# Fourier mixing and a gated feed-forward block on one core: the order of the opening, and the first chunk's second matmul

## The chip, the cores and the metric

The kernel runs on one core of a Trainium2 chip. The core has a matmul engine (PE, with a separate row PEld for loading its stationary operand), a vector engine (DVE), an activation engine (ACT), a general-purpose engine (POOL) and a queue engine (SP) that here only starts transfers. Each engine works through its own list of instructions in order and waits on semaphores for the others. Transfers between the chip's memory and the on-chip buffers are started from SP's and POOL's lists. The metric is the device time of one execution in microseconds (us); lower is better.

## The reference

The input `x` has 8 batches of 3008 positions with 256 channels, in fp32. The reference takes the real part of a Fourier transform along both axes and feeds every position through a gated block with 1536 hidden units:

```python
X = np.fft.fft(x, axis=1)
X = np.fft.fft(X, axis=2)
y = X.real.reshape(24064, 256)
g = y @ w_gate
gelu = 0.5 * g * (1.0 + erf(g / sqrt(2)))
out = (gelu * (y @ w_val)) @ w_out
```

## The kernel before

**Transform.** The 3008 positions are split as 94 x 32. `x` of a batch is loaded twice: forward (rows 32 p + j) and mirrored (an indirect gather, "M" below). A fold adds and subtracts the two (`fold_ops`, L216 to L220), so that only 17 columns j are left; a piece (j0, nj) is nj of them. Stage 1 (`s1`, L467) multiplies the folded pieces with a matrix G of cosines and sines, four groups of j by two halves, and copies each result to A (L473 on ACT, L475 on DVE). `ch` (L489) multiplies A with signed identities II and gives Z; `tp_e`, `tp_o` and `tp_y` (L544, L549, L569) multiply Z with a small table TP and give EO (even and odd parts) and EB. The channel transform is not done on the data: it is folded into the weights by `make_w` (L417), which multiplies the raw weights with a table CW, and `make_yw` adds a rank-one term.

**Feed-forward.** A batch has three chunks of up to 512 column pairs; each chunk has 12 blocks of 128 hidden units. One block is one slot of the order written out in `feed()`, so there are 8 x 3 x 12 = 288 slots. In slot i PE does the two gate matmuls of block i (`l1_gate`), one more for the mirrored gate of block i - 1 (`l1_gate2`), the value matmul of block i (`l1_value`) and the second one of block i - 1 (`l1_value2`), all at L622. ACT applies the gelu twice (L638, L647). DVE makes `ve` (L656), the product for the forward sign (L667) and `v` (L669). POOL makes the product for the mirrored sign (L671). Both products go to `h`.

**Layer 2.** `l2_piece(ci, sub, sign, f0)` (L695) is four matmuls over four hidden blocks; a chunk has 4 sub-blocks x 2 signs x 3 = 24 pieces. The six pieces of a sub-block share the one PSUM buffer with tag "o"; after the sixth, ACT copies it out (L714) and SP stores it. The list `pend` holds the pieces of the chunk just finished. Two are taken in each slot of the next chunk: the first after the value matmul, the second after `l1_value2`.

**Order.** Nothing is scheduled by a planner: the program order is written by hand. `opening()` holds the constants, the loads and the first batch up to the first gate. `plan()` gives for each slot the further work: `fill` (stage 1, `ch`, `tp`, loads, `make_w`) comes at the end of a slot, `pool` (folds of the next batch on POOL) before `l1_value2`. In the first chunk `fill` makes the rest of the weights in slots 0 to 7 and the rest of the first batch's transform in slots 7 to 16. `second_x` and its followers start the loads of the second batch in slots 0 to 5; folds of the second batch on POOL begin in slot 6. The loads of the third batch are started in slots 18 and 19.

**The lines that the change touches.** In `opening()` SP loads the forward part of `x` for j = 9 to 16 and 0 as fp32 (`stage`); POOL's list has first its index and constant rows, then the gathers and the casting loads of `x`, then w and w_out. DVE and ACT make the tables: G's phases (L314 to L261) and sines (L328 to L338), CW (L343 to L359), the identities (L363 to L366, on ACT) and TP (L371 to L388). `warm(n)` puts n matmuls without use on PE (L757). `keep2` is the factor with which `make_w` writes a third form of the odd gate weights ("minus", L427).

Of the kernel before, what the change touches and what calls it, by code (L numbers as in the profile page):

```python
# [28 lines left out]
def kernel(  # L29
# [17 lines left out]
    NK = 24  # L47
# [51 lines left out]
    def stage_tile():  # L99
        return work([NPX, 9, C], FP32, "h", 2, "x_stage")  # L100
# [89 lines left out]
    def fold_ops(b, j0, nj, eng):  # L190
# [3 lines left out]
        def fwd(c0, pat):  # L194
            if b == 0 and j0 not in range(1, 9):
                return _sub(stage[0], [[C, nj]] + pat, (j0 - 9 if j0 else 8) * C + c0, part_num=NP)
            if half:
                return _sub(xb[b], [[C, nj]] + pat, j0 * C + c0, part_num=NP)
            return _sub(raw_tile(FORWARD), [[C, nj]] + pat, j0 * C + c0, part_num=NP)
# [35 lines left out]
    sc_g = const_pool.tile([128, 2], FP32)  # L235
    row_j = const_pool.tile([128, NJ], FP32)
    row_k = const_pool.tile([128, NK], FP32)
    row_c, eye = (const_pool.tile([128, 128], FP32, name=f"row{i}") for i in range(2))
    par = const_pool.tile([1, 5, 128], FP32)
    one = const_pool.tile([1, 1], FP32)  # L240
# [8 lines left out]
    rd = work([128, 2 * NGP], FP32, "Z", 1, "rd")  # L249
# [5 lines left out]
    col_i = const_pool.tile([128, 2], FP32)  # L255
# [7 lines left out]
    def index_consts(i):  # L263
        idx, base = ((idx_x, NP - 1), (idx_0, NP))[i]
        nc.gpsimd.iota(col_i[:, i : i + 1], pattern=[[0, 1]], base=base, channel_multiplier=-1, **IOTA)
        if i:
            nc.gpsimd.memset(col_i[0:1, i : i + 1], 0.0)
        nc.gpsimd.tensor_scalar(idx, col_i[:, i : i + 1], 0.0, None, op0=ALU.max)

    def pool_consts():  # L270
# [4 lines left out]
        nc.gpsimd.iota(row_c, pattern=[[1, 128]], base=0, channel_multiplier=0, **IOTA)  # L275

    def pool_consts2():

        nc.gpsimd.iota(
            par[:, 0, :], pattern=[[1, 16], [0, 2], [32, 2], [0, 2]], base=1, channel_multiplier=0, **IOTA)
        for r, v in ((120, 0.0), (122, 32.0), (126, 16.0)):
            nc.gpsimd.memset(par[:, 0, r : r + 2], v)
        nc.gpsimd.iota(row_t, pattern=[[1, K1]], base=0, channel_multiplier=0, **IOTA)

    def vec_fills():
        nc.vector.memset(G[:, 0, 2 * NK :], 0.0)
        nc.vector.memset(G[:, 16, 0 : 2 * NK], 0.0)
        nc.vector.memset(one, 1.0)  # L290
# [13 lines left out]
    def vec_consts():  # L304
# [3 lines left out]
        nc.vector.tensor_scalar(col_e, col_h, -1.0, 1.0, op0=ALU.mult, op1=ALU.add)  # L308
        nc.vector.tensor_scalar(sc_g[:, 1:2], col_h, -TWO_PI, None, op0=ALU.mult)
        nc.vector.tensor_scalar(sc_g[:, 0:1], col_h, TWO_PI, -TWO_PI, op0=ALU.mult, op1=ALU.add)  # L310

    def g_phases():
        f, r, d = (_sub(t, [[1, 2 * NGP]], 0, part_num=NP) for t in (ff, rr, rd))
# [7 lines left out]
        nc.vector.tensor_scalar(f[:, NK:NGP], f[:, NGP + NK :], 0.25, None, op0=ALU.add)  # L321
        nc.vector.tensor_scalar(f[:, 0:NK], f[:, NGP : NGP + NK], 0.125, None, op0=ALU.add)
        reduced(d, r, f)

    def g_sin(j0, nj):
# [7 lines left out]
    def g_sin_ends():  # L333
# [3 lines left out]
        for h in range(2):  # L337
            nc.scalar.activation(  # L338
                _sub(G, [[1, NK]], h * NK), _sub(rd, [[1, NK]], 0, part_num=NP),
                AF.Sin, scale=sc_g[:NP, h : h + 1])  # L340

    def cw_phases():
        nc.vector.tensor_scalar(col_n0, col_p, 1.0 / C, None, op0=ALU.mult)  # L343
        nc.vector.tensor_scalar(cf[:, 0:128], row_c, col_n0, 0.25, op0=ALU.mult, op1=ALU.add)
        nc.vector.tensor_scalar(cf[:, 128:256], row_c, col_n0, 0.5, op0=ALU.mult, op1=ALU.add)
        reduced(cd[:, :], cr[:, :], cf[:, :])

    def cw_sin():
        nc.scalar.activation(_sub(CW, [[256, 2], [1, 128]], 0), cd[:, :], AF.Sin, scale=-TWO_PI)

    def cw_rest():


        nc.scalar.activation(CW[:, 0, 0, 0:1], col_e, AF.Copy)
        nc.scalar.activation(CW[:, 1, 0, 0:1], col_h, AF.Copy)
        for i, sign in enumerate((1.0, -1.0)):
            nc.scalar.activation(
                _sub(CW, [[256, 2], [2, 64]], 128 + i), _sub(CW, [[256, 2], [2, 64]], i), AF.Copy, scale=sign)
        nc.scalar.activation(CW[:, 1, 1, 0:1], col_h, AF.Copy)  # L359

    def identities():

        nc.scalar.activation(eye, row_c, AF.Abs, scale=-1.0, bias=col_p)  # L363
        nc.scalar.activation(II[:, 0, 0, :], eye, AF.Relu, scale=-1.0, bias=1.0)
        for i, sign in ((1, 1.0), (2, 1.0), (3, -1.0)):
            nc.scalar.activation(II[:, i // 2, i % 2, :], II[:, 0, 0, :], AF.Copy, scale=sign)  # L366

    def t_columns():
        ps = psum("v")
        for i in range(5):  # L370
            nc.tensor.matmul(ps[:, i : i + 1], par[:, i, :], one, start=True, stop=True)  # L371
        nc.vector.tensor_copy(parc, ps[:, 0:5])
        nc.vector.tensor_scalar(parc[:, 0:1], parc[:, 0:1], 1.0 / K1, None, op0=ALU.mult)

    def t_phases():
        k1 = _sub(row_t, [[1, K1]], 0)
        for i in range(2):
            nc.vector.tensor_scalar(
                tf[:, i * K1 : (i + 1) * K1], k1, parc[:, 0:1], parc[:, 1 + i : 2 + i], op0=ALU.mult, op1=ALU.add)
# [5 lines left out]
    def t_write():  # L385
        for d in range(2):
            nc.scalar.activation(
                _sub(TP, [[128, 2], [1, K1]], d * K1), _sub(tf, [[K1, 2], [1, K1]], 0), AF.Copy,  # L388
                scale=parc[:, 3 + d : 4 + d])

    row_t = const_pool.tile([128, K1], FP32)
    sink = const_pool.tile([1, 1], BF16, name="sink")

# [10 lines left out]
    def load_wo(q):  # L404
        n = NFC // 4
# [5 lines left out]
    def make_w(i, f0, n, parts=(0, 1), engine="A"):  # L411

        def run():
# [12 lines left out]
            if i == 0 and 1 in parts:  # L426
                nc.scalar.activation(W["g", "M"][:, f0 : f0 + n], ps[:, m - n : m], AF.Copy, scale=keep2)  # L427
# [190 lines left out]
    def ffn_work(b):  # L618
# [60 lines left out]
        def l2_piece(ci, sub, sign, f0):  # L679
            def run():  # L680
# [12 lines left out]
                half = slice(sign * C, (sign + 1) * C)  # L693
                for fc in range(f0, f0 + L2P):
# [4 lines left out]
                        start=(fc == 0),  # L699
                        stop=(fc == NFC - 1),  # L700
                    )
# [28 lines left out]
    def opening():  # L730
        stage[0] = stage_tile()
        xb[0] = xb_tile(0)
        for j0, nj, at in ((9, 8, 0), (0, 1, 8)):
# [4 lines left out]
        pool_consts2()  # L738
        index_consts(0)
        cast_mirror(0, 9, 8)  # L740
        cast_forward(0, 1, 8)
        cast_mirror(0, 5, 4)
        cast_mirror(0, 1, 4)
        index_consts(1)
        cast_mirror(0, 0, 1)
        for f0, n in ((0, 256), (256, 256), (512, 1024)):
            load_w(f0, n)
        for q in range(4):
            load_wo(q)
        idle = gelu_tile()[:, 0, :]  # L750
        nc.vector.memset(idle, 0.0)
# [11 lines left out]
        def stage1(jg):  # L763
            s1(0, jg, 0)()
            s1(0, jg, 1, "V" if jg == 0 else "A")()

        warm(11)
        vec_consts()
        g_phases()
        vec_fills()  # L770
        cw_phases()
        g_sin(9, 7)
        g_sin_ends()
        g_sin(1, 8)
        cw_sin()
        t_columns()
        t_phases()
        t_sin()
        warm(10)
        nc.vector.tensor_scalar(keep2, col_p, 1.0, None, op0=ALU.min)  # L780
        nc.vector.tensor_scalar(keep2, keep2, -2.0, None, op0=ALU.mult)
        gelu_table()
        t_write()
        identities()
        cw_rest()
        fold_piece(9, 4)
        stage1(2)
        warm(4)
        fold_piece(13, 4)
        fold_piece(5, 4)  # L790
        warm(2)
        stage1(1)
        warm(3)
        fold_piece(0, 1)
        stage1(3)
        warm(2)
        fold_piece(3, 2)
        fold_piece(1, 2)
        stage1(0)
        make_w(0, 0, 256, engine="V")()  # L800
        ch(0, 0)()
        ch(0, 1, "V")()
        make_w(1, 0, 256, engine="V")()
        tp_e(0, 0)()
        tp_o(0, 0, "V")()

# [94 lines left out]
    def feed():  # L901
# [6 lines left out]
        pend, before = [], None  # L908
# [59 lines left out]
```

## Time and profile before

| | us |
|---|---|
| median of 3 runs | 633.9 (632.75 to 634.33) |
| time of the profiled execution | 633.91 |
| its span, first to last instruction | 632.1 |
| PE busy in it | 618.9 |
| first gate matmul | 20.47 |
| start of slot 12 (the first gate of the second chunk) | 44.86 |

The profile records one execution. Its page gives the busy time of each engine and, followed back from the last instruction, the chain of work and waits that ended last. The timeline lists instructions by engine with their start and duration and, in brackets, how long the engine was idle before and what released it. Instructions of one engine overlap by some tenths of a microsecond, so the distance from start to start is what one costs in a row.

### The profile page before, as it was taken

The page shows a single profiled execution, that of the slowest core. Times are in us where ns is not written, and L with a number is a line of the kernel's source. Part 1 is how long each engine was busy: PE and PEld are TensorE (multiplying, and loading weights), DVE is VectorE, ACT ScalarE, POOL GpSimd, SP SyncE. Part 2 cuts the span into 40 slices and gives each one's busy share as a digit, 9 for nine tenths or more (in the row PEclk, how much of TensorE's full clock was granted, in tenths as well). Part 3 has the DMA queues.
Part 4 walks back from the last instruction along what each step waited for, and adds up shares of the span by engine and source line. Part 5 has one row for each costly group of instructions (what it writes and reads, how often), then busy time and mean ns, then how long its engine had stood idle before and what let it go on. Part 6 is the DMA issues. An engine that isn't in the chain of part 4 may idle for free.

```text
span 632.1 us, 13032 instructions
## 1 busy us (share of the span) xinstructions
PE 618.9 (98%) x4285; PEld 407.4 (64%) x4285; DVE 580.9 (92%) x937; ACT 432.7 (68%) x855; POOL 505.7 (80%) x511
## 2 busy tenths in 40 slices
PE   7999999999999999999999999999999999999997
PEld 3446666666666666666666666666666666666666
DVE  7698889999899989999999999999999999999992
ACT  6787777666766667666776767766776766666651
POOL 8599799989997998879998799968988555555651
PEclk8999999999999999999999999999999999999999
DMA  8931925535454352633635325633222232221123
GB/s 152 179 61 26 250 63 147 139 99 138 121 146 107 91 140 65 167 84 100 156 93 155 93 66 138 153 92 104 57 53 57 75 104 54 52 51 38 43 51 80
DMA packets 51994, 63.84 MB, mean 101 GB/s; under 512 B 7783, under 2 KB 47194, under 8 KB 49530
## 3 DMA queue, kind: packets, MB, share of 16 engines
q1 hardware_dynamic: 45238, 47.23, 28.9%
q0 software_dynamic: 6096, 15.29, 11.5%
q8 instruction: 33, 0.54, 0.3%
q10 hardware_dynamic: 592, 0.49, 0.3%
q14 instruction: 35, 0.29, 0.1%
HBM read 38.86 MB, written 29.38 MB: 108 GB/s over the span
## 4 chain that ended last, share of the span: by engine, by line
PE 87%; DMA 4%; DVE 3%; POOL 2%; ACT 2%; issue 1%; POOLq 0%; DVEq 0%; ACTq 0%
PE ps_o L695 36%; PE ps_g L622 27%; PE ps_v L622 17%; DMA Z_sb<-z 3%; PE ps_dft L508 2%; PE ps_dft L544 2%; POOL h_sb L671 1%; DVE v_sb L669 1%; DMA xb<-in_x_dram,idx 1%; DVE h_sb L667 1%; PE ps_o L757 1%; PE ps_dft L574 1%; ACT gelu_sb L638 1%; DVE ve_sb L656 1%; PE ps_g L695 0%
## 5 line engine op out<-in xcount | busy, mean ns | idle before, releaser
L671 POOL TENSOR_TENSOR h_sb<-gelu_sb,v_sb 128x512 bf16<-128x512 bf16 (+1 forms) x288 | 328.7, 1144 | 106.3 <-DVE v_sb L669 92.0
L695 PE MATMUL ps_o<-Wo_sb,h_sb 128*128 128x256 bf16 (+1 forms) x2232 | 334.9, 273 | 1.0 <-POOL h_sb L671 1.0
L695 PEld LDWEIGHTS <-h_sb 128*128 128x128 bf16 (+1 forms) x2304 | 228.8, 100 | 112.5 <-POOL h_sb L671 2.7
L656 DVE SCALAR_TENSOR_TENSOR ve_sb<-EB_sb,yw,ps_v 128x512 f32<-128x512 bf16 (+1 forms) x288 | 212.1, 737 | 32.8 <-PE ps_v L622 29.0
L638 ACT ACTIVATE gelu_sb<-ps_g 128x512 bf16<-128x512 f32 (+1 forms) x288 | 169.6, 589 | 96.4 <-PE ps_g L622 93.0
L622 PE MATMUL ps_g<-EO_sb,W_sb 128*128 128x512 bf16 (+1 forms) x864 | 231.2, 375 | 2.7 <-ACT gelu_sb L647 2.0
L622 PE MATMUL ps_v<-EO_sb,W_sb 128*128 128x512 bf16 (+1 forms) x576 | 214.4, 375 | 0.5 <-ACT W_sb L423 0.5
L667 DVE TENSOR_TENSOR h_sb<-gelu_sb,ps_v 128x512 bf16<-128x512 bf16 (+1 forms) x288 | 195.0, 677 | 1.1 <-ACT gelu_sb L647 0.7
L669 DVE SCALAR_TENSOR_TENSOR v_sb<-ve_sb,ps_v 128x512 f32<-128x512 f32 (+1 forms) x288 | 192.6, 669 | 0.0
L622 PEld LDWEIGHTS <-W_sb 128*128 128x128 bf16 x1440 | 136.8, 98 | 82.3 <-issue 4.2
L647 ACT ACTIVATE gelu_sb<-ps_g 128x512 bf16<-128x512 f32 (+1 forms) x288 | 169.1, 587 | 0.0
L714 ACT ACTIVATE out_sb<-ps_o 128x512 f32<-128x512 f32 x92 | 54.9, 597 | 36.1 <-PE ps_o L695 36.0
L224 POOL TENSOR_TENSOR eo_sb<-ab_sb 94x512 bf16<-94x512 f32 (+1 forms) x60 | 66.6, 1110 | 0.1
L554 ACT ACTIVATE EO_sb<-ps_dft 128x512 bf16<-128x512 f32 (+1 forms) x44 | 26.0, 590 | 22.5 <-PE ps_dft L544 20.5
L511 ACT ACTIVATE S_sb<-ps_dft 96x512 bf16<-96x512 f32 x48 | 28.2, 587 | 11.3 <-PE ps_dft L508 11.3
L217 POOL TENSOR_TENSOR ab_sb<-x_raw,x_raw 94x508 f32<-94x508 f32 (+1 forms) x30 | 33.0, 1101 | 0.0
L220 POOL TENSOR_TENSOR ab_sb<-x_raw,x_raw 94x508 f32<-94x508 f32 (+1 forms) x30 | 32.9, 1096 | 0.0
L158 POOL DMA_INDIRECT x_raw<-in_x_dram,idx x18 | 17.0, 945 | 2.8 <-issue 0.6
L508 PE MATMUL ps_dft<-eo_sb,G 94*96 94x256 bf16 x102 | 19.2, 274 | 0.0
L544 PE MATMUL ps_dft<-TP,Z_sb 128*128 128x128 bf16 (+1 forms) x188 | 18.2, 218 | 0.5 <-DVE Z_sb L496 0.5
L544 PEld LDWEIGHTS <-Z_sb 128*128 128x128 bf16 x192 | 14.5, 98 | 2.4 <-DVE Z_sb L496 0.7
L757 PE MATMUL ps_o<-gelu_sb 128*128 128x512 bf16 x32 | 11.1, 498 | 1.2 <-DVE col L305 1.2
(128 smaller groups left out, 173.5 us busy)
## 6 DMA issues: line engine op xcount, KB each, us to landing
out_dram<-out_sb SPq DMA_DIRECT2D x361, 64.0 KB
x_raw<-in_x_dram SPq DMA_DIRECT2D x10, 768.0 KB
Z_sb<-z SPq DMA_DIRECT2D x6, 768.0 KB
z<-S_sb SPq DMA_DIRECT2D x6, 576.0 KB
EB_sb<-yrow SPq DMA_DIRECT2D x14, 128.0 KB
x_raw<-in_x_dram SPq DMA_DIRECT2D x2, 640.0 KB
z<-S_sb SPq DMA_DIRECT2D x6, 192.0 KB
EB_sb<-yrow SPq DMA_DIRECT2D x7, 120.2 KB
```

The source lines that it names most:

```text
L217: eng.tensor_tensor(ab(0, 1, up), fwd(1, up), mir(255, down), op=ALU.add)
L224: eng.tensor_tensor(_sub(eo, [[C, nj], [1, 128]], j0 * C + g * 128), ab(0, 0, [[1, 128]]), ab(1, 0, [[1, 128]]), op=op)
L544: nc.tensor.matmul(ps[:, o : o + n], st["Z"][:, pair, g * 128 : g * 128 + 128], _sub(TP, [[1, n]], g * 128), start=True, stop=True)
L622: nc.tensor.matmul(ps[:, :n], W[nm, part][:, fs], src, start=start, stop=stop, **kw)
L638: nc.scalar.activation(gl[:, 0, :n], pg[:, :n], AF.Gelu)
L647: nc.scalar.activation(_sub(gl, [[-1, n]], TOK + n - 1), pg[:, :n], AF.Gelu)
L656: nc.vector.scalar_tensor_tensor(ve[:, :n], EB_bufs[b][:, c0 : c0 + n], yw[:, fc : fc + 1], pv[:, :n], op0=ALU.mult, op1=ALU.add)
L667: nc.vector.tensor_tensor(st["h"][:, fc, 0, :n], gl[:, 0, :n], pv[:, :n], op=ALU.mult)
L669: nc.vector.scalar_tensor_tensor(_sub(vv, [[-1, n]], n - 1), ve[:, :n], 2.0, pv[:, :n], op0=ALU.mult, op1=ALU.subtract)
L671: nc.gpsimd.tensor_tensor(st["h"][:, fc, 1, :n], gl[:, 1, :n], vv[:, :n], op=ALU.mult)
L695: nc.tensor.matmul(pso[:m, half], st["h"][:, fc, sign, h0 : h0 + m], Wo_sb[:, fc, :], start=(fc == 0), stop=(fc == NFC - 1),)
L714: nc.scalar.activation(_sub(osb, [[1, 2 * C]], 0, part_num=m), pso[:m, :], AF.Copy)
```

## The change

In `opening()`, POOL's list has the index row and the gather M(9,8) directly after four small constants. The index is made by an integer iota without the clamping operation (a fill with zero covers the two last rows). After the gather come the forward loads (13,4), which was SP's, and (1,8), both casting to bf16, then the rows `row_c`, `par`, `row_t`, then the other gathers, with (0,1) ahead of (1,4). w is loaded in four pairs instead of three, w_out in two halves instead of four quarters. SP loads j = 9 to 12 and 0 only.

DVE fills the constant tiles first. The cosine rows of G and of CW are taken from |phase| - 1/4 instead of from a second reduced phase; the absolute value for CW is taken by ACT. The identities are written by DVE with a comparison. Several small operations change engine: CW's and TP's last writes go from ACT to DVE, the copies of the t columns and the t phases from DVE to ACT. The t columns' matmuls stand before all warm-up matmuls, which are 12, 5 and 1 instead of 11, 10, 4, 2, 3 and 2. The sine table is loaded by a call of its own.

Stage 1's copies are given to other engines, the fold (3,2) and (1,2) become one (1,4), the first gate weights are copied by ACT, and the second `make_w` and the "minus" copy come after `tp_o`.

In `feed()` the first six pieces of the first chunk's layer 2 (sub-block 0) are put into slots 6, 7, 10, 11 and 13. In slot 12 no piece is taken, and the other 18 pieces follow two by two from slot 14, so the last ones are in slot 22. In sub-block 0 the first piece of the second sign does not set the start flag.

```diff
-        for j0, nj, at in ((9, 8, 0), (0, 1, 8)):
+        for j0, nj, at in ((9, 4, 0), (0, 1, 4)):
...
         pool_consts()
-        pool_consts2()
         index_consts(0)
         cast_mirror(0, 9, 8)
+        cast_forward(0, 13, 4)
         cast_forward(0, 1, 8)
+        pool_consts2()
         cast_mirror(0, 5, 4)
-        cast_mirror(0, 1, 4)
         index_consts(1)
         cast_mirror(0, 0, 1)
-        for f0, n in ((0, 256), (256, 256), (512, 1024)):
+        cast_mirror(0, 1, 4)
+        for f0, n in ((0, 256), (256, 256), (512, 512), (1024, 512)):
             load_w(f0, n)
-        for q in range(4):
+        for q in range(2):
             load_wo(q)
...
-        warm(11)
+        vec_fills()
         vec_consts()
         g_phases()
-        vec_fills()
+        vec_consts2()
+        identities()
+        par_n1()
+        g_rows(9, 7)
         cw_phases()
-        g_sin(9, 7)
-        g_sin_ends()
-        g_sin(1, 8)
+        g_ends()
+        cw_magnitude()
+        t_columns()
+        g_rows(1, 8)
+        t_phases()
         cw_sin()
-        t_columns()
-        t_phases()
+        warm(12)
+        fold_piece(9, 4)
+        t_reduced()
         t_sin()
-        warm(10)
...
         gelu_table()
-        t_write()
-        identities()
-        cw_rest()
-        fold_piece(9, 4)
-        stage1(2)
-        warm(4)
         fold_piece(13, 4)
+        s1(0, 2, 0, "V")()
+        s1(0, 2, 1, "V")()
+        cw_rest()
+        t_write()
+        warm(5)
         fold_piece(5, 4)
-        warm(2)
-        stage1(1)
-        warm(3)
+        s1(0, 1, 0)()
+        s1(0, 1, 1)()
         fold_piece(0, 1)
-        stage1(3)
-        warm(2)
-        fold_piece(3, 2)
-        fold_piece(1, 2)
-        stage1(0)
-        make_w(0, 0, 256, engine="V")()
+        s1(0, 3, 0)()
+        warm(1)
+        fold_piece(1, 4)
+        s1(0, 3, 1, "V")()
+        s1(0, 0, 0)()
+        s1(0, 0, 1, "V")()
+        minus = []
+        make_w(0, 0, 256, m_at=minus)()
         ch(0, 0)()
         ch(0, 1, "V")()
-        make_w(1, 0, 256, engine="V")()
         tp_e(0, 0)()
         tp_o(0, 0, "V")()
+        make_w(1, 0, 256, engine="V")()
+        minus[0]()
...
     def identities():
-        nc.scalar.activation(eye, row_c, AF.Abs, scale=-1.0, bias=col_p)
-        nc.scalar.activation(II[:, 0, 0, :], eye, AF.Relu, scale=-1.0, bias=1.0)
-        for i, sign in ((1, 1.0), (2, 1.0), (3, -1.0)):
-            nc.scalar.activation(II[:, i // 2, i % 2, :], II[:, 0, 0, :], AF.Copy, scale=sign)
+        nc.vector.tensor_scalar(
+            _sub(II, [[128, 3], [1, 128]], 0), _sub(row_c, [[0, 3], [1, 128]], 0), col_p, None, op0=ALU.is_equal)
+        nc.vector.tensor_scalar(II[:, 1, 1, :], row_c, col_p, -1.0, op0=ALU.is_equal, op1=ALU.mult)
...
     def t_phases():
         k1 = _sub(row_t, [[1, K1]], 0)
         for i in range(2):
-            nc.vector.tensor_scalar(
-                tf[:, i * K1 : (i + 1) * K1], k1, parc[:, 0:1], parc[:, 1 + i : 2 + i], op0=ALU.mult, op1=ALU.add)
+            nc.scalar.activation(
+                tf[:, i * K1 : (i + 1) * K1], k1, AF.Identity, scale=parc[:, 0:1], bias=parc[:, 1 + i : 2 + i])
+
+    def t_reduced():
         reduced(td[:, :], tr[:, :], tf[:, :])
...
+        first = works[0]
+        sooner = {6: [first[0]], 7: [first[3]], 10: [first[1]], 11: [first[4]], 13: [first[2], first[5]]}
+        works[0] = first[6:]
         for i, (parts, fc) in enumerate(blocks):
             if fc == 0 and i:
                 assert not pend
                 pend = list(works[i // NFC - 1])
+            two = sooner.pop(i, []) if i <= NFC + 1 else [pend.pop(0) for _ in range(2) if pend]
...
-            if pend:
-                pend.pop(0)()
+            if two:
+                two.pop(0)()
```

## The prediction

> **What bounds the kernel now.** I read the page's busy line and chain first, then the timeline of the first 85 us engine by engine, since every edit is there.
>
> ```profile
> PE 618.9 (98%) x4285; PEld 407.4 (64%) x4285; DVE 580.9 (92%) x937; ACT 432.7 (68%) x855; POOL 505.7 (80%) x511
> PE 87%; DMA 4%; DVE 3%; POOL 2%; ACT 2%; issue 1%; POOLq 0%; DVEq 0%; ACTq 0%
> ```
>
> PE sets the end: once it runs full, the time left is its remaining work. What can move is when that begins, and what PE has done by then. The timeline (start, us, engine, line, operation; in brackets the idle time before) shows the opening:
>
> ```profile
> 10.02 0.19 DVE L216 TENSOR_TENSOR eo_sb<-x_stage,xb 94x8 bf16<-94x8 f32 x1 [0.89 <-DMA xb<-in_x_dram,idx]
> ...
> 14.02 0.16 DVE L216 TENSOR_TENSOR eo_sb<-x_stage,xb 94x2 bf16<-94x2 f32 x1 [0.33 <-DMA xb<-in_x_dram,idx]
> ...
> 17.09 0.56 DVE L475 CAST A_sb<-ps_v 128x384 bf16<-128x384 f32 x1 [1.55 <-PE ps_v L467]
> ...
> 20.47 0.38 PE L622 MATMUL ps_g<-EO_sb,W_sb 128*128 128x512 bf16 x1
> ```
>
> The mirror gathers set the pace to 14.3; the last stage-1 copy ends at 17.65 (call this A); the first gate starts at 20.47. Slots 0 to 3 then run on ACT, slots 4 to 11 on DVE. One row is decisive, PE in slot 14:
>
> ```profile
> 51.64 0.49 PE L695 MATMUL ps_o<-Wo_sb,h_sb 128*128 128x256 bf16 x3
> 52.77 0.28 PE L695 MATMUL ps_o<-Wo_sb,h_sb 128*128 128x256 bf16 x1 [0.63 <-POOL h_sb L671]
> ```
>
> The sixth layer-2 piece waits with its last matmul for POOL's product of slot 11; from 52.77 PE has no hole until 80.92. POOL's own timeline:
>
> ```profile
> 33.15 1.16 POOL L671 TENSOR_TENSOR h_sb<-gelu_sb,v_sb 128x512 bf16<-128x512 bf16 x1 [0.44 <-DVE v_sb L669]
> ...
> 49.34 1.15 POOL L671 TENSOR_TENSOR h_sb<-gelu_sb,v_sb 128x512 bf16<-128x512 bf16 x1
> 50.45 1.14 POOL L220 TENSOR_TENSOR eo_sb<-xb 94x508 bf16<-94x508 bf16 x1
> 51.56 1.15 POOL L671 TENSOR_TENSOR h_sb<-gelu_sb,v_sb 128x512 bf16<-128x512 bf16 x1
> ```
>
> Between the product of slot 3 (33.15, waiting for `v`) and the end of that of slot 11 (52.72) POOL never idles over 0.2 us: nine products 10.4, two gathers 1.9, the folds of the second batch 8.9 less overlaps. That date hangs on `v` of slot 3 and on nothing PE does.
>
> [...] warm-up matmuls start 0.427 apart up to 5.1 us and 0.216 apart later, and in the table of busy time by stretch (length, then PE, PEld, DVE, ACT, POOL busy, clock, DMA share, GB/s) a stretch with PE busy for 1.42 of 3.40 us is followed by one at 0.51:
>
> ```profile
> 8.50:11.90 3.40, 1.42 (x13) 0.64 (x12) 2.44 (x9) 2.93 (x7) 2.95 (x7) 1.00 1.04 204
> 11.90:15.30 3.40, 3.34 (x16) 1.52 (x15) 2.89 (x14) 2.95 (x13) 3.40 (x5) 0.51 1.11 153
> ```
>
> [...] one piece that waits holds everything behind it, as at 52.77. [...] the gather's packets and the stage load did not overlap here, and less stage load remains.
>
> **The change, part by part.**
>
> *Gather first.* POOL loses ahead of it the 1.38 us iota, row_c, row_t, three memsets and a conversion, and keeps four small operations to about 1.58; with the 0.28 gap it issues at 1.86, not 4.26. It then landed 5.7 later: 7.6, not 10.0. The forward casts move behind it, M(5,4) from 6.85 to about 5.9, the last x piece to about 12.7 (was 14.0), and the weights follow 1.3 earlier. The weights are hidden and stay so: the first w block landed at 14.64 and was used at 16.9; without that cover each us late would delay the gate by one. POOL now issues 16 loads, not 15 (w in four pairs, out-weights in two halves); from the ninth on each waits for the landing of the one eight before. Behind them in POOL's queue stands only the first product (26.30), some 7 us after the last issue before. The row and par iotas now come behind three loads, at about 5.0 and 5.4, before their first readers (6.5 on ACT, 5.7 and 6.4 on DVE). SP's queue has half the stage load and nothing new.
>
> *Who uses it.* DVE, by spacing of the same rows: fills 1.0 now lead (to 2.05), column constants 0.67, then 0.60 for the products, 0.27, about 0.37 (half of 0.62), two two-input passes 0.55 each, 0.36, 0.13: G's phases end at 5.5 (were 4.9). Identities (five ACT rows, 1.4 us, gone): no row shows the compare; the 128-element rows (0.2 each) bound it at 0.45 for both from below, the 384-element row that took 0.65 beside a POOL iota at 0.85 from above; I take 0.65, and 0.35 for the par repairs. The par row is ready at 6.8 (its last fill was at 5.84). Only then PE makes the t columns, with no matmul before it, since the 11 early warm-ups are gone. Ten passes at 0.11 took 1.2 warm; cold they take 1.2 to 2.4, I take 1.8: 8.6. ACT: copy 0.2, two G sines 0.5 each (now queued ahead of the t phases), t phases 2 x 0.2: 10.2. DVE reduces them (0.5) with fold (13,4) queued behind: fold (9,4) ends at 8.9 but (13,4) (0.77) only at 11.5. PE's 12 warm-ups stand ahead of stage 1 and begin at 8.6: at 0.216 to 0.427 each they end at 11.2 to 13.7, I take 12.2. Stage 1 plus 0.37: 12.55. Then DVE alone: two copies 0.94, CW and TP 1.1 (moved there from ACT), fold (5,4) 0.77, (0,1) 0.48, (1,4) 0.77, copies 0.47 + 0.56: A at 17.6. The bounds are 16.3 and 19.6. Change of A: -0.05.
>
> *A to slot 0.* Before, W's copy and the minus copy stood ahead of Z: A + 2.8 to the gate. After: chain to Z on ACT A + 1.2, on DVE A + 1.75; transform, EO copy A + 2.65; minus (0.47) A + 3.0; the value-weight matmuls (0.44) wait for it, and the gate stands behind them in PE's order: E at A + 3.5, O at 3.7, gelu 4.1. `yw` waits for the weights' DVE copy (0.68, to 4.3), the y transform follows at 4.45, its ACT copy runs from 4.87 to 5.47, and the next weight matmuls wait for both. The ACT row that starts the slots' work (W's copy, 22.87 = A + 5.22 before) comes at A + 5.5: +0.28. Slots 0 to 3 have the same ACT work, so `v` of slot 3, and with it POOL's slot-11 product, come 0.25 later: 52.95.
>
> *Layer 2.* Six pieces of 0.437 us move: one each to slots 6, 7, 10, 11, two to 13; slot 12 and slot 23 lose two each. Slots 6 to 11 have room: PE work 1.08 + 0.2 to 0.9 + piece, sum 10.8, against DVE's 6 x 1.86 + 1.2 = 12.4; with that room gone the four pieces would cost 1.75 here. The changed start flag adds no instruction. In slot 11 the piece waits some 0.5 for POOL's slot-7 product (44.75), covered since DVE lags PE by 1.6 there. But the sixth piece now stands in slot 13, where PE arrives about 49.1. Both dates move by the 0.25, so it waits about 3.6 us, and behind it in PE's order stand the fills of slot 13, the gate and value of slot 14. So at the moment when before only later work remained, PE still owes what before it had done: fills 0.61 and slot 14's five matmuls 1.08, together 1.69. DVE, which needs slot 14's value, stands too. No piece is cheaper; the idle time has only moved. Added: +1.69 (bounds: 0.6, if POOL's queue runs 1 us earlier than the rows say, and 2.0).
>
> *Slot 23.* Slots 14 to 22 thus run 2.54 later, and slot 23 gives back 0.87. The loads for the third batch are issued in slots 18 and 19, and POOL's next fold waited for them (75.97, 1.80 idle); the product behind it made PE wait in slot 26:
>
> ```profile
> 80.92 0.28 PE L695 MATMUL ps_o<-Wo_sb,h_sb 128*128 128x256 bf16 x1 [0.32 <-POOL h_sb L671]
> ```
>
> That date moves by the whole 2.54, PE arrives 0.87 less late: 0 to 0.87 more waiting; I take 0.6.
>
> Sum: -0.05 + 0.28 + 1.69 + 0.6 = +2.5. The profiled execution was 633.91 (span 632.1), the median 633.9: predicted span 634.6, time 636.4.
>
> **Rivals.** (1) Not slower: the four pieces fill idle PE time for good, 4 x 0.437 = -1.75; with +0.25 of opening 632.4. For: PE does wait on DVE in slots 6 to 11. Against: needs POOL's slot-11 product by 49.2, 3.5 us earlier, and its queue is unchanged and full. (2) The 2.4 us of the gather reach A: -2.4 + 0.28 + 1.69 + 0.6: 634.1. For: DMA was the releaser. Against: DVE's queue, which takes over. (3) A cold PE: the warm-ups finish at 13.7 or later, or a window after them is granted half, with fewer warm-ups (18, were 32): A + 2: 638.4. For: 11.9:15.3 did so with more of them. [...]
>
> **Numbers.** Forecast 45% (its own range 635.4 to 637.4), (1) 12%, (2) 20%, (3) 23%. About 0.3%, 1.9 us, is what a measurement of this kernel can tell: 632.0 to 635.8 is no change. Slower: 36 of the forecast's 45, all 23 of (3), 1 of (2): 60%. Faster: 5 of (1), 2 of (2): 7%. Same: 33%. Leaving out most of (1) and the top of (3): 633.4 to 638.9.
>
> **What would show it.** First gather issued near 1.9; t columns near 6.8; fold (13,4) later than 10.5 with DVE idle before the t reduction, released by ACT; A within 1 us of 17.6. The sixth piece in slot 13 with a wait of about 3.5 us for POOL's product, DVE idle about 2.5 there; a wait of about 1 at slot 26. Wrong if POOL's slot-11 product comes well before 51, or if PE meets no long wait there.

## The result, and the profile after

The changed kernel takes 643.3 us (642.9 to 643.68) beside 634.1 us for the kernel before on the same chip: a ratio of 1.0149, 95% interval 1.0132 to 1.0167. It is 9.2 us slower; 2.5 were forecast, and the range ended at 638.9. The profiled execution took 643.68, its span is 641.9.

The page's busy line and the shares of its chain, after:

```profile
PE 614.9 (96%) x4222; PEld 407.8 (64%) x4271; DVE 581.4 (91%) x946; ACT 431.8 (67%) x848; POOL 504.4 (79%) x509
PE 86%; DMA 4%; DVE 3%; POOL 2%; ACT 2%; issue 2%; SPq 1%; POOLq 0%; ACTq 0%; DVEq 0%
```

PE is not busy for longer and its end comes 9.8 us later, so it stands longer. (The 4.0 us that it is busy less are in part a gap in the trace: after, 49 matmul records are missing, 4,222 beside 4,271 weight loads; before, both counts are 4,285.) SP's queue, which was not among the shares before, has 1% of the chain.

Where the time is lost is read best from the slots. The table sets the start of a slot (its first gelu) in a profiled execution against the same slot of the kernel before, in us. The last columns are the median of all runs of that kernel, the kernel before beside it, and the ratio. The lower rows are the experiments told below. The execution of the kernel before against which the slots are set took 633.9, 0.7 to 1.1 more than its medians in the lower rows, and those of e1 and e4 (635.0 and 635.5) were among the fastest of theirs, so the slots of a row don't add up to its last columns.

| kernel | slot 0 | 13 | 14 | 27 | 136 | 287 | median | before | ratio (95%) |
|---|---|---|---|---|---|---|---|---|---|
| after | 2.80 | 2.75 | 7.27 | 6.51 | 7.37 | 9.83 | 643.3 | 634.1 | 1.0149 (1.0132 to 1.0167) |
| e1 | -0.86 | -0.25 | 3.39 | 1.89 | 1.45 | 1.02 | 637.5 | 632.9 | 1.0080 (1.0063 to 1.0097) |
| e2 | 2.47 | 2.66 | 2.66 | 3.98 | 4.01 | 6.59 | 639.8 | 632.9 | 1.0105 (1.0087 to 1.0122) |
| e3 | 2.80 | 2.75 | 7.47 | 6.41 | 6.08 | 5.49 | 639.1 | 632.9 | 1.0096 (1.0079 to 1.0113) |
| e4 | -0.91 | -0.97 | 3.76 | 2.75 | 1.78 | 1.64 | 637.1 | 632.9 | 1.0063 (1.0047 to 1.0080) |
| e5 | 0.53 | 0.48 | 0.34 | 2.94 | 2.82 | 2.24 | 635.3 | 633.0 | 1.0033 (1.0024 to 1.0042) |
| e6 | 1.23 | 1.17 | 5.87 | 5.18 | 5.07 | 4.67 | 638.9 | 633.0 | 1.0089 (1.0064 to 1.0113) |
| e7 | 0.00 | 0.19 | 0.19 | 0.22 | -0.64 | -1.21 | 632.9 | 633.0 | 1.0009 (0.9991 to 1.0027) |
| e9 | 0.28 | 0.29 | 0.29 | 1.35 | 1.29 | 2.87 | 636.8 | 633.0 | 1.0062 (1.0043 to 1.0080) |
| e10 | 1.79 | 1.73 | 5.37 | 4.34 | 3.71 | 3.52 | 637.4 | 632.8 | 1.0071 (1.0057 to 1.0085) |
| e11 | -0.57 | -0.63 | -0.77 | -0.05 | -0.39 | -0.85 | 633.7 | 632.8 | 1.0015 (1.0000 to 1.0030) |
| e12 | 1.01 | 1.20 | 1.20 | 1.47 | 1.34 | 0.76 | 634.5 | 632.8 | 1.0019 (1.0004 to 1.0033) |
| e13 | 0.09 | 0.28 | 0.28 | 0.54 | 0.17 | -0.40 | 633.4 | 633.2 | 1.0003 (0.9994 to 1.0012) |

The row "after" shows three places: the opening (2.8 by slot 0), slot 13 (a jump of 4.5, of which 0.8 comes back by slot 27), and a slow rise behind it (6.51 to 9.83), where not one instruction of the program is different.

**The opening.** The timeline after:

```profile
7.00 2.26 PE L387 MATMUL ps_v<-one,par 1*128 1x1 f32 x10 [7.00 <-DVE par L288]
...
8.58 0.19 DVE L216 TENSOR_TENSOR eo_sb<-x_stage,xb 94x8 bf16<-94x8 f32 x1 [0.93 <-DMA xb<-in_x_dram,idx]
...
9.19 5.30 PE L788 MATMUL ps_o<-gelu_sb 128*128 128x512 bf16 x12
...
14.28 0.53 PE L493 MATMUL ps_g<-G,eo_sb 94*128 94x96 bf16 x4
...
14.84 0.56 DVE L501 CAST A_sb<-ps_g 128x384 bf16<-128x384 f32 x1 [2.36 <-PE ps_g L493]
...
17.08 0.18 DVE L216 TENSOR_TENSOR eo_sb<-xb 94x8 bf16<-94x8 bf16 x1
...
19.58 0.56 DVE L501 CAST A_sb<-ps_v 128x384 bf16<-128x384 f32 x1
...
23.91 0.38 PE L648 MATMUL ps_g<-EO_sb,W_sb 128*128 128x512 bf16 x1
```

The gather's first fold starts at 8.58, 1.4 sooner than before. But PE is cold, at half its later pace: the t columns take 2.26 (1.27 before), the 12 warm-ups 5.30, 0.427 each from start to start where a warm PE takes 0.216, and stage 1, whose input was folded by 9.95, stands behind them in PE's order until 14.28. DVE waits for it with two copies, and the fold (5,4), which needs nothing from PE, stands behind these copies in DVE's order until 17.08. A ends at 20.14.

**Slot 13.** PE and POOL in the timeline, and the table of busy time by stretch (length, then PE, PEld, DVE, ACT, POOL busy, clock, DMA share, GB/s):

```profile
52.32 1.15 POOL L697 TENSOR_TENSOR h_sb<-gelu_sb,v_sb 128x512 bf16<-128x512 bf16 x1
...
53.52 0.28 PE L722 MATMUL ps_o<-Wo_sb,h_sb 128*128 128x256 bf16 x1 [1.02 <-POOL h_sb L697]
...
54.54 1.15 POOL L697 TENSOR_TENSOR h_sb<-gelu_sb,v_sb 128x512 bf16<-128x512 bf16 x1
...
55.74 0.28 PE L722 MATMUL ps_o<-Wo_sb,h_sb 128*128 128x256 bf16 x1 [1.94 <-POOL h_sb L697]
```

```profile
52.50:55.90 3.40, 0.44 (x4) 0.24 (x4) 1.68 (x3) 0.00 (x0) 3.40 (x5) 1.00 0.00 0
55.90:59.30 3.40, 3.18 (x16) 1.92 (x16) 1.11 (x2) 2.17 (x4) 2.17 (x2) 0.51 0.19 46
```

The sixth piece waits for the products of slots 10 and 11, 2.96 in all. That was expected. The second table shows what was not: PE is busy for 0.44 of 3.40 us, and in the next stretch, full of work, its clock is 0.51. The half-clock window lasts from 55.97 to 59.38, 3.41 us, and half of that, 1.7, is an estimate of what it costs. The kernel before had one in its opening (0.51 from 11.90); this one is in the middle of the kernel.

**The later batches.** One row of the view of PE's waits, after and then before (total, times, longest):

```profile
PE ps_dft L600 <- DMA Z_sb<-z: 3.9, 4, 1.0
```

```profile
PE ps_dft L574 <- DMA Z_sb<-z: 0.5, 2, 0.2
```

Four times PE stands about 1 us for the read of Z. In SP's queue that read stands behind four stores. SP in the timeline, for the batch whose read was issued at 292.03 (284.88 before), after and then before:

```profile
288.77 3.15 SPq L642 DMA_DIRECT2D out_dram<-out_sb  x4
```

```profile
282.37 2.40 SPq L616 DMA_DIRECT2D out_dram<-out_sb  x4
```

The same four issues take 0.75 longer. One of them takes 1.33, where 0.59 is usual. In the trace, 28 of SP's DMA issues take over 0.8 us, 7 in the kernel before, and 23 of the 28 overlap a packet of 16 KB of the queue "instruction". The view of the transfers from 288.0 to 292.5 has such a packet, and before there is none in the stretch that answers to it:

```profile
q8 instruction: 1, 0.02, 1.3%
```

Each of the two executions has 33 of these packets, 0.54 MB. PE's weight loads and matmuls together are 8,542 after and 8,570 before (twice 4,271 and twice 4,285). What the packets carry, and what sets their times, the traces don't show. The suspicion, the author's and not more at this point, is that 28 PE instructions fewer (14 warm-ups with their weight loads) have moved the packets, for the rest of the program, onto the stores ahead of the read of Z.

### The profile page after: what moved, and what is told of

Read it like the earlier page. It is cut to its first block, busy times and chain, and to the rows that moved or that the text cites. A ratio compares the mean times of both kernels' runs of the same rounds, so it can differ in the third digit from the quotient of the medians.

```text
span 641.9 us, 12956 instructions
## 1 busy us (share of the span) xinstructions
PE 614.9 (96%) x4222; PEld 407.8 (64%) x4271; DVE 581.4 (91%) x946; ACT 431.8 (67%) x848; POOL 504.4 (79%) x509
## 4 chain that ended last, share of the span: by engine, by line
PE 86%; DMA 4%; DVE 3%; POOL 2%; ACT 2%; issue 2%; SPq 1%; POOLq 0%; ACTq 0%; DVEq 0%
PE ps_o L722 36%; PE ps_g L648 26%; PE ps_v L648 17%; DMA Z_sb<-z 3%; PE ps_dft L534 2%; PE ps_dft L570 1%; POOL h_sb L697 1%; PE ps_o L788 1%; DMA EO_sb<-yrow 1%; PE ps_dft L515 1%; ACT gelu_sb L664 1%; PE ps_dft L600 0%; ACT gelu_sb L673 0%; SPq L642 0%; PE ps_g L722 0%
## 5 line engine op out<-in xcount | busy, mean ns | idle before, releaser
L648 PE MATMUL ps_g<-EO_sb,W_sb 128*128 128x512 bf16 (+1 forms) x816 | 228.6, 376 | 4.8 <-ACT gelu_sb L673 1.5
L534 PEld LDWEIGHTS <-G 94*96 94x96 bf16 x102 | 11.2, 124 | 0.6
```

What stands on the lines that cost most here:

```text
L534: nc.tensor.matmul(ps[:96, q * C : (q + 1) * C], G[:, j, :], _sub(eo, [[1, C]], j * C), start=(j == js[0]), stop=(j == js[-1]))
L648: nc.tensor.matmul(ps[:, :n], W[nm, part][:, fs], src, start=start, stop=stop, **kw)
```

## The experiments

All kernels but e2 and e9 have the old number of PE instructions.

**e1 and e2: each half of the change alone.** e1 is the kernel before with the new `feed()` (and the start flags that belong to it); e2 is the changed kernel with the old one.

For e1, on the kernel before:

```diff
+        sooner = {6: [first[0]], 7: [first[3]], 10: [first[1]], 11: [first[4]], 13: [first[2], first[5]]}
+        works[0] = first[6:]
...
+            two = sooner.pop(i, []) if i <= NFC + 1 else [pend.pop(0) for _ in range(2) if pend]
```

For e2, on the changed kernel:

```diff
-        sooner = {6: [first[0]], 7: [first[3]], 10: [first[1]], 11: [first[4]], 13: [first[2], first[5]]}
-        works[0] = first[6:]
...
-            two = sooner.pop(i, []) if i <= NFC + 1 else [pend.pop(0) for _ in range(2) if pend]
```

> The kernel before, with the sooner layer-2 pieces alone; the opening is the old one and PE has the old count of instructions. Theory: the sixth piece waits about 3 us in slot 13 for POOL's products, PE loses half its clock in the window after it, and the kernel takes +3 to +4 us (637 to 638); no wait of PE for Z later on. Rival (the wait alone costs, as the prediction had it): +1.7 us (635.8). Rival (the stall appears only behind the new opening): +0 to +0.5 us.

> The changed kernel with the old order of layer 2: the opening alone, with the 28 PE instructions fewer. Theory: slot 0 about +2.8 us late as in the changed kernel, no stall in slot 13, and four PE waits of about 1 us for Z in the later batches: +6 us (640). Rival (the later waits belong to the stall in layer 2): +3 us (637).

e1 took 4.6 us more (637.5), e2 7.0 (639.8). The stall of 3.0 is there behind the old opening too, so the third reading of e1 is out. e1's five executions suggest two parts of its cost: 635.0 at a mean clock of 0.999, and 637.5, 637.9 and 638.6 at 0.993 to 0.995, where one half window is 0.0027 of the mean clock and at most 1.7 us. One more, of 636.0 at 1.000, doesn't fit, and the mean clock alone tells little: the executions of the kernel before have 0.995 to 1.000 at much the same time. When the clock was halved is known for the profiled one alone, that of 635.0. There it stayed full behind the stall. Counted in steps of 3.41 us from the start of its clock record (these records last whole multiples of 3.41: 3.41, 6.83, 10.24, 40.96), the stall is spread over two steps, in which PE was busy for 1.92 and 1.74 us, where the stretch ahead of the changed kernel's half window has 0.44 of 3.40. That this is why the clock stayed full is not shown:

```profile
47.75:51.16 3.41, 1.92 (x11) 0.80 (x9) 3.41 (x6) 1.14 (x3) 3.41 (x5) 1.00 0.00 0
51.16:54.57 3.41, 1.74 (x14) 1.25 (x16) 0.72 (x2) 1.45 (x3) 3.41 (x5) 1.00 0.00 0
```

In e2 the four waits for Z are there (3.5 us) without the stall in slot 13: they belong to the opening or to the number of instructions.

**e3 and e9: PE's number of instructions.** e3 gives the changed kernel 14 matmuls of one element at PE's start, when PE is idle. e9 takes 14 warm-ups from the kernel before.

For e3, on the changed kernel (`pad(n)` is n matmuls of 1x1 on `idle`):

```diff
+        pad(14)
         vec_fills()
```

For e9, on the kernel before:

```diff
-        warm(10)
+        warm(3)
...
-        warm(4)
+        warm(2)
...
-        warm(2)
+        warm(1)
         stage1(1)
-        warm(3)
+        warm(1)
...
-        warm(2)
```

> The changed kernel with 14 matmuls of one element at PE's start, in time that PE is idle: PE has as many instructions as in the kernel before, [...]. Theory (instruction packets stretch SP's stores ahead of the read of Z): the waits for Z fall from 4 us to under 1 us in all, and the time by 2.5 to 3.5 us, to 640 to 641, with slots 0 to 26 as in the changed kernel. Rival (the stretched stores have another cause): 643, waits for Z as they were.

> The kernel before with 14 of its 32 warm-ups less: PE has the changed kernel's count of instructions, and nothing else is changed. Theory (the places of the instruction packets stretch SP's stores): 25 or more of SP's DMA issues take over 0.8 us, PE waits four times about 1 us for Z, and the time is 2.5 to 4.5 us above the kernel before, plus what the opening loses on a colder PE (0 to 3 us): 635.5 to 640. Rival (the packets have no part in it, and the changed kernel's other timing makes the stores slow): under 10 such issues, and nothing lost behind the opening.

e3 starts slot 0 at the same 2.80, and from slot 27 to 287 it loses nothing (6.41 to 5.49), where the changed kernel loses 3.3. Its time is 6.2 us over the kernel before in place of 9.2. Stretched issues: 7. The wait for Z is gone, the view of the transfers from 287.5 to 291.5 has no 16 KB packet, and the four stores are back at 2.40:

```profile
288.58 2.40 SPq L642 DMA_DIRECT2D out_dram<-out_sb  x4
```

e9 is the other direction. Nothing is lost up to slot 23 (0.30), then 2.6 us to slot 287. Of these, 1.05 come at slot 27: a store's issue of 1.89 at 62.58 holds SP's loads of the third batch back (issued from 65.38, before from 63.78), POOL's fold waits 2.86 for them (1.80 before), and PE waits for POOL. There are 27 stretched issues, 24 of them beside a 16 KB packet. The four stores ahead of the same read as above, and PE's waits for Z:

```profile
282.65 3.65 SPq L616 DMA_DIRECT2D out_dram<-out_sb  x4
```

```profile
PE ps_dft L574 <- DMA Z_sb<-z: 2.9, 4, 1.1
```

So 14 matmuls more or fewer, worth nothing by themselves, switch about 3 us on and off. That the number of PE instructions does it is shown, for these two numbers: e3 and e9 alter no other engine's program, and all eleven traces with the old number have 5 to 9 stretched issues, all three with the smaller one 27 or 28. Why an issue on SP slows beside the packet, and how PE's number of instructions bears on it, is not shown.

**e4, e6, e12: PE's clock in the opening.** e4 puts 14 full warm-ups ahead of the t columns. e6 has 26 small matmuls at the start and leaves out the 12 warm-ups behind the t columns. e12, on e7 below, has 11, 8 and 12 warm-ups in place of 14, 12 and 5.

For e4 and then e6, on the changed kernel:

```diff
+        warm(14)
         vec_fills()
```

```diff
+        pad(26)
         vec_fills()
...
-        warm(12)
```

For e12, on e7:

```diff
-        warm(14)
+        warm(11)
...
-        warm(12)
+        warm(8)
...
-        warm(5)
+        warm(12)
```

> The changed kernel with 14 full warm-up matmuls ahead of the t columns; PE's count of instructions is the old one. Theory (PE is cold through the opening): the t columns take 1.3 us in place of 2.26 and come before 6 us, the 12 warm-ups run at full clock and end before 12 us, the last A copy ends 1 to 2 us sooner (18 to 19), and [...] the time is 638 to 639.5. Rival (DVE's folds and their data set A, not PE's clock): the last A copy within 0.5 us of 20.1, and the time that of the run with the small matmuls.

> The changed kernel without the 12 warm-ups behind the t columns (26 matmuls of one element at PE's start in place of 14 and of the 12). Theory (stage 1 waits behind the cold warm-ups): stage 1's first matmul at 12.0 or sooner in place of 14.28, on a cold PE; the last A copy 0.5 to 1.5 us sooner than 20.1, as the matmuls behind are slower; time 638 to 639. Rival (without the warm-ups the clock comes later still, and that costs more than the queue): the last A copy 0 to 1 us later, time 639 to 641.

> The changed kernel with the old order of layer 2, and 11 warm-ups ahead of the t columns, 8 behind them, 12 in place of 5 behind stage 1's first group (32 in all, as many as in the kernel before). Theory (what is left of the new opening's loss is half-clock windows that follow PE's waits in it): no half window between 8 and 20 us in most runs, slot 0 at -1 us or sooner against the kernel before, time 631.5 to 632.3, faster than both kernels. Rival (DVE's folds set the opening, and the half windows hide beside them): slot 0 within 0.4 us of the kernel before, time 632.5 to 633.5.

The timeline of e4:

```profile
7.00 1.24 PE L387 MATMUL ps_v<-one,par 1*128 1x1 f32 x10 [1.15 <-DVE par L288]
8.18 2.76 PE L788 MATMUL ps_o<-gelu_sb 128*128 128x512 bf16 x12
10.78 0.34 PE L493 MATMUL ps_g<-G,eo_sb 94*128 94x96 bf16 x4
...
15.86 0.56 DVE L501 CAST A_sb<-ps_v 128x384 bf16<-128x384 f32 x1
```

The t columns don't start sooner (they wait for `par`), but take half, the warm-ups too, and A ends at 16.42, more than the 1 to 2 us sooner that were expected and 1.2 before the old A. Slot 0 moves from +2.80 to -0.91 (the same opening gives -0.57 in e11, and 0.00 and 0.53 in e7 and e5, where a half window falls into it). The time is 4.2 us over the kernel before, 2.0 better than e3; the two intervals just meet. In e6 stage 1 starts at 9.31, on a cold PE, and A ends at 17.60: the queue of warm-ups alone was worth 2.5 us of A. Slot 0 gained 1.6, but little of it lasts: the ratio is 1.0089 beside e3's 1.0096. This PE was granted half its clock once more, from 16.24 to 19.65, and slots 13 to 27 cost it 4.0 us where they cost e3 3.7. e12 met neither theory. With only 11 warm-ups ahead PE stands 1.8 us before the t columns and then gets two half windows in a row:

```profile
7.60:11.00 3.40, 3.40 (x12) 1.90 (x12) 1.77 (x6) 2.66 (x9) 3.09 (x5) 0.50 1.08 196
11.00:14.40 3.40, 3.40 (x16) 1.58 (x15) 2.70 (x12) 1.86 (x4) 3.40 (x6) 0.50 1.22 167
```

Its 12 warm-ups behind stage 1's first group run at half clock and hold the second group; A ends at 18.35.

**e10, e5, e11: the sixth piece.** e10 (on e3) puts 12 matmuls whose result isn't used ahead of it, so that PE is busy where it stood. e5 and e11 (on e4) move it later: first in slot 14, and second in slot 14 with all that follows half a slot or a slot later.

For e10, on e3, with `pad(2)` in place of `pad(14)`:

```diff
+        w_busy = W['g', 'E'][:, 0:512]
...
+                if i == 13:
+                    fps = psum('dft')
+                    for _ in range(12):
+                        nc.tensor.matmul(fps[:, :], Wo_sb[:, 0, 0:128], w_busy, start=True, stop=True)
                 two.pop(0)()
```

For e5, on e4, and then e11, on e5:

```diff
-        sooner = {6: [first[0]], 7: [first[3]], 10: [first[1]], 11: [first[4]], 13: [first[2], first[5]]}
-        works[0] = first[6:]
+        sooner = {6: [first[0]], 7: [first[3]], 10: [first[1]], 11: [first[4]], 13: [first[2]]}
+        works[0] = first[5:]
```

```diff
-        works[0] = first[5:]
+        works[0] = [lambda: None] + first[5:]
```

> The kernel with the small matmuls at PE's start (2 in place of 14), and 12 matmuls of 128x512, whose result is not used, ahead of the sixth piece in slot 13, so that PE is busy where it stood. Theory (PE's standing there brings the half-clock window): PE's wait for POOL's products falls from 3.0 us to about 0.5, no window of half clock between 50 and 62 us, slot 14 starts no later, and slot 27 starts 1 to 2 us sooner than with the small matmuls alone (6.41 us behind the kernel before): time 637 to 638. Rival (the window comes whatever PE does): a half window as before, time 639 or, with the filler behind time, more.

> The changed kernel with 14 warm-ups ahead of the t columns (as in the run before), and the sixth piece of layer 2 one slot later, first in slot 14. Theory (the wait for POOL's product, and the half-clock window that can follow it, are the loss in layer 2): PE waits under 0.5 us for POOL there, no window of half clock is granted between 45 and 65 us in any run, and the time is 1.5 to 3.5 us under that of the run before (633.5 to 635.5). Rival (the early pieces hold DVE's work back, wherever the sixth stands): the time within 0.7 us of that run.

> The changed kernel with 14 warm-ups ahead of the t columns; the sixth piece of layer 2 half a slot later again, second in slot 14, and the rest of the pieces from slot 15 on, two a slot. Theory (the sixth piece stands while POOL, busy without a gap, is behind): PE waits under 0.8 us for POOL there in place of 1.7, and slots 14 to 27 lie 0.5 to 1.5 us nearer to the kernel before than with the piece first in slot 14: time 634 to 635. Rival (early pieces are no gain wherever the sixth stands, since DVE has no free time in slots 6 to 13): the same 635.3 as there, or more.

e10's stretches, and what is left of PE's wait:

```profile
50.60:54.00 3.40, 3.23 (x17) 1.58 (x17) 2.56 (x5) 0.47 (x1) 3.40 (x4) 1.00 0.00 0
54.00:57.40 3.40, 2.83 (x24) 1.91 (x23) 1.53 (x3) 2.17 (x4) 3.09 (x4) 1.00 0.08 19
```

```profile
54.76 0.28 PE L722 MATMUL ps_o<-Wo_sb,h_sb 128*128 128x256 bf16 x1 [0.57 <-POOL h_sb L697]
```

No half window, and e10 is 1.6 us nearer to its kernel before than e3 is (1.0071 beside 1.0096), with more work on PE. In the profiled executions 1.0 of this is there at slot 0 already (1.79 beside 2.80), since e10's clock turned full at 12.90, among its 12 warm-ups behind the t columns, which took 4.58 and not 5.30, and e3's only at 14.58; what set that is open. The stall is better read from slot 13 to 27. There e1 and e10, with no half window, lose 2.1 and 2.6, and the changed kernel, e3, e4 and e6, with one each, lose 3.7 to 4.0: a half window behind the stall costs 1 to 1.9. All four executions of e10 have a mean clock of 0.999 or more, those of e3 0.994 to 0.997. e10's slot 13 takes 6.20 us, as in e1's execution, and 7.29 in e3's: slot 14 still comes no sooner than POOL's product, the clock is kept. e5 took 1.9 us off e4 and e11 3.3 (from 1.0063 to 1.0033 and 1.0015), about as much as expected, but not in the way expected. PE still waits in both:

```profile
53.50 0.28 PE L722 MATMUL ps_o<-Wo_sb,h_sb 128*128 128x256 bf16 x1 [1.68 <-POOL h_sb L697]
...
54.47 0.60 PE L722 MATMUL ps_o<-Wo_sb,h_sb 128*128 128x256 bf16 x4 [0.47 <-ACT out_sb L742]
```

```profile
52.41 0.28 PE L722 MATMUL ps_o<-Wo_sb,h_sb 128*128 128x256 bf16 x1 [1.48 <-POOL h_sb L697]
```

The likely difference is what stands behind the wait. In the changed kernel slot 14's gate and value, which DVE and POOL live on, come after it. In e5 (the first two lines) the second value matmul still does, and the next pieces follow so closely that PE waits three more times, 1.9 us in all, for ACT's copy of the one buffer "o"; from slot 13 to 27 it loses 2.5. In e11 (the last line) all five matmuls of slot 14 have been done, no such wait is left, and from slot 15 to 26 each of its slots has the length that it has in the kernel before; from slot 13 to 27 it loses 0.6. The early pieces then bring nothing, and the likely reason is seen in the kernel before: from 35.1 to 52.1 DVE was busy for all of the 17.0 us and PE for 15.6, so PE's work put there bought no time.

**e7 and e13: what is left.** e7 is e4 with the old `feed()`, so its edit of the changed kernel is that of e2 and this:

```diff
+        warm(14)
         vec_fills()
```

e13 is e7 with DVE's order changed: the fold (5,4) ahead of the first two copies of stage 1, `cw_rest` and `t_write` behind the last fold.

```diff
         fold_piece(13, 4)
+        fold_piece(5, 4)
         s1(0, 2, 0, "V")()
         s1(0, 2, 1, "V")()
-        cw_rest()
-        t_write()
         warm(5)
-        fold_piece(5, 4)
...
         fold_piece(1, 4)
+        cw_rest()
...
         s1(0, 0, 1, "V")()
+        t_write()
```

> The changed kernel with 14 warm-ups ahead of the t columns and the old order of layer 2. Theory (the whole of the loss is the cold PE, the stall in layer 2 and the places of the instruction packets): slots 0 to 287 start about 0.9 us sooner than in the kernel before, time 632 (631 to 632.5). Rival (the opening has a debt that comes due later, in the slots of the weights and of the second batch): 633 to 635.

> The changed kernel with the old order of layer 2, 14 warm-ups ahead of the t columns, and on VectorE the fold of pieces 5 to 8 ahead of the first two copies of stage 1, and the edits of CW and TP behind the last fold. Theory (VectorE, busy without a gap from 10 us on, sets the last A copy once PE is warm): the last A copy ends at 15.5 to 16.0 in place of 16.42, slot 0 at -0.6 to -1.4 us against the kernel before, time 631.5 to 632.5, a little faster than both kernels. Rival (the gain is lost again to a half-clock window in the opening or to the chain behind A): 632.7 to 634.

e7 is level with the kernel before (1.0009, interval 0.9991 to 1.0027; one of its twelve executions, of 638.3, stands apart from the others, 632.0 to 634.5): warm-ups ahead, the old layer 2 and the old number of PE instructions take back the whole of the 9.2 us. In its profiled execution A ends at 16.42, but a half window from 15.81 to 19.22 eats the gain by slot 0. e13 is level too (1.0003): the fold (5,4), moved forward, waits 0.65 for its gather, to 12.13, and A ends at 16.66, just before a half window from 16.82 to 20.24. No version beat the kernel before by more than the measurement can tell.

In the order in which the edits were undone, the 9.2 us are: 3.0 by the number of PE instructions (after to e3), 2.0 by the cold PE in the opening (e3 to e4), 4.3 by the new layer-2 order, that is the stall in slot 13 with the half windows that can follow it (e4 to e7). Each is a difference of two medians and good to about 1 us. The parts are not independent: taken alone out of the changed kernel, the stall is worth 2.2 (e2).

## Why the prediction was wrong

The profiled executions give the sum to set beside the prediction's: A +2.49, A to slot 0 +0.31, slots 0 to 10 +0.49, slots 10 to 27 +3.22, the rest +3.32; together 9.83. The prediction had -0.05, +0.28, nothing, +1.69 and +0.6, and nothing. So it falls short by 7.3 us: 2.5 in A, 0.5 in the first slots, 0.9 from slot 10 to 27, and 3.3 in the rest.

*Gather first, and A.* This step failed. The gather was issued at 1.90 (1.86 forecast), the t columns began at 7.00 (6.8), the fold (13,4) stood behind the t reduction. But the t columns took 2.26 where 1.8 was taken, and the warm-ups 0.427 each from start to start, where a middle was taken: stage 1 came at 14.28, not 12.2, and this is 2.1 of the 2.5 us. The rest is stage 1 on a PE still cold (0.56 to the first copy, not 0.37) and the edits of CW and TP on DVE (1.30, not 1.1). The late end of the warm-ups, 13.7, was reckoned from the middle case of the t columns; with both slow it is 14.3, and A's late bound of 19.6 was passed by 0.5. Rival (3) was this mechanism with nearly the right size for A (+2), but priced as another case with the rest unchanged. e4 and e6 show the cause: with PE warm the same edits end A at 16.42, near the early bound of 16.3, and cold but without the 12 warm-ups at 17.60. The gather itself took 6.7 to its fold, not 5.7; behind the warm-ups this cost nothing.

*A to slot 0.* +0.28 forecast, +0.31 measured.

*Slots 0 to 10.* "Slots 6 to 11 have room" put the early pieces at nothing. They cost 0.3 by slot 10: of the 0.49, e2 with the old order has 0.19.

*Layer 2.* The mechanism was right: same place, same releaser, a wait of 2.96 (3.6 forecast), DVE idle for 2.67 there (2.5). In e1's execution, where the clock was not halved there, slots 10 to 27 cost 1.59; the term was 1.69. (The 2.54 for slots 14 to 22 is about this and the 0.87 of two pieces, without the opening's 0.25; in e1 slots 18 to 23 lie 2.25 to 2.45 further behind than slot 10.) What failed is a missing term. The prediction showed a half window in the opening and did not ask what a stall of 3 us does to the clock behind it. In the changed kernel slots 10 to 27 cost 3.22, 1.6 more than in e1's execution and 1.1 more than in e10's, where PE was kept busy and the window did not come.

*Slot 23.* The 0.87 is given back (7.36 to 6.51), the 0.6 of new waiting did not come: POOL's fold of the third batch starts at 81.49 without a wait, since its three gathers landed 6.4 to 10.3 us after their issue, not 10.9 to 11.5 as before. This term was wrong, and in the kernel's favour. (For the 1.80 of idle time at 75.97 the timeline names DVE, not a load; that it was the load is the likelier reading, since in e9 and e11 the same fold's wait is put down to it.)

*What was not in the sum.* "Once PE runs full, the time left is its remaining work" was taken as true of the last 550 us, and nothing was booked there. They cost 3.3. The prediction counted PE's 14 warm-ups fewer as nothing, while in this kernel the number of slow issues on SP goes with PE's number of instructions (28 after, 7 in e3, 27 in e9): with them put back as matmuls of one element (e3), nothing is lost there.

*The rivals.* (1) and (2) are out: POOL's product of slot 11 came at 55.7, and of the gather's time nothing reached A in the changed kernel.

## What to carry to other kernels

Ask of each forecast wait of PE whether a half-clock window can come behind it, and price the window (1 to 1.9 us here) with the wait: the stall of 3 us drew one in four traces of five, waits of 1.7 and 1.5 (e5, e11) drew none. Ask also what stands behind the waiting instruction, since in e11 a wait of 1.5 us, with all that follows, cost 0.6. Where one uncertain duration feeds another, add their slow cases before calling the sum a bound. A change in the number of instructions of an engine early in a long unrolled program can move time in parts that it doesn't touch (3.0 us here, after to e3), so compare with the number held constant (some matmuls of one element will do) before blaming the edit.

## What the runs showed of the hardware that was not expected

In the trace after, 23 of the 28 slow DMA issues on SP (0.9 to 1.9 us in place of 0.59) overlap a packet of 16 KB of the queue "instruction", in flight for 0.9 to 1.6 us. The traces before and after have 33 such packets each. A slow issue met 23 of them after, 24 in e9, both with the smaller number of PE instructions, and 4 to 6 in those with the old number (4 in the kernel before). A half window did not need an idle stretch ahead of it, and PE's busy time there alone doesn't decide it: stretches of 3.41 us in which PE was busy for 1.30 (e6, from 12.83), 1.53 (e5, from 11.94) and 2.20 us (e13, from 13.41) were followed by a half window, the two of 1.92 and 1.74 in e1 were not. The mean granted clock of single executions of one kernel went from 0.992 to 0.999 (e4), and the time from 638.0 to 633.9 with it; one of these eight was traced, so what differed between them is not shown. Ten fp32 passes of one column took 1.24 us on a warm PE (e4) and 2.26 on a cold one (after).
